# A fused softmax-convolution and cosine FFN on one core: an f32r product moved in every second pair, activation steps of a softmax put in other pairs, and a result tile for each bank at the end

## The chip, the core and the metric

The kernel runs on one core of one Trainium2 chip. The time is device microseconds of one execution, and the median of several runs counts. Engines are named as in the profile: PE (TensorE) with its weight loads PEld, ACT (ScalarE), DVE (VectorE), POOL (GpSimd), SP (the queue that issues DMAs).

## What is computed

For each of 8 sequences of 4,096 tokens with 192 features, a softmax over 7 taps for each of 8 heads weighs the 7 last rows of `x`; the result goes through an FFN with 2,048 hidden features whose activation is `h * cos(h)`. All is f32.

```python
w = exp(weight_gen - max); w = w / (sum(w) + 1e-9)      # softmax over 7 taps, per token and head
x = einsum('bshk,bskhg->bshg', w, windows_of_7_rows(x)) # 32768 x 192
h = x @ w_in                                            # 192 -> 2048
out = (h * cos(h)) @ w_out                              # 2048 -> 192
```

## The kernel before, in words

**Blocks and pairs.** The 32,768 tokens are 64 blocks of 512 (128 partitions times R = 4 rows). The 16 chunks of 128 hidden features make 8 pairs a block, so the main loop (L658) runs over 512 pairs `i`, one in each turn, with `j = i - 8` for the pair whose hidden part is consumed. One turn of the loop is called a period here. What each engine does in a period, and in which order, is the order of the code: the last lines of the kernel chain the instructions of each engine in program order.

**The products on PE.** Each f32 operand is cut in two: an f32r part (`x_hi`, `wa_hi`, `ghi`, `wo`) and a bf16 rest (`x_lo`, `wa_lo`, `glo`), and a product is the sum of the f32r product and of bf16 products of the rests. The contraction over 192 is cut into 128 + 64, and matmuls with 64 rows stand in twos on the two halves of the array. In a period PE does, by function:
- F, `ffn_in_first(i)` (L391): three products of 512 columns into a PSUM tile `h`: `x_lo`, `x_b` (bf16), then `x_hi` (f32r).
- O, `ffn_out(j)` (L468): 16 f32r matmuls `acc<-wo,ghi` of 384 columns, then two transposes (`transpose_row`, L374, `acc<-ident,xa`) of rows of a later block, then 16 bf16 matmuls `acc<-wo_b,glo` of 192 columns.
- the second products, `ffn_in_second(i)` (L406): four bf16 products and two f32r products into `h`.

In even pairs the order is F, O, second. In odd pairs (L682) it is O up to half of its bf16 matmuls (`rest=False`: the `ghi`, the transposes, 8 of the `glo`), then F, then the other 8 `glo` (`rest=True`), then second. `h` has three PSUM buffers, so F of pair `i` needs that `dve_lo(i - 3)` has read the buffer's last content. `acc` has one buffer of two banks; a sum in it takes four periods, k = 0 to 3 with k = i mod 4.

**The other engines.** For each pair ACT makes `turn` from `h` (L427), the cosine (L435) and `ghi` (L445); DVE makes the fraction (L431), the product (L438) and `glo` (L449). `evacuate` (L501) stands behind the products of a period: for k = 1 ACT copies the transposed row out of `acc` (`xrow`, L507) and zeroes its place (L508), for k = 3 it copies the whole `acc` to `part` (L513). The next O that writes `acc` waits for that copy, or for the zeros. In even periods ACT also rounds a row to `x_hi` (L357); POOL makes its `x_b` and `x_lo` (L359, L362).

**The background.** POOL computes the softmax-weighted rows (`attention`, L303), two or three instructions a period. The softmax of 16 rows (4 blocks) is a generator (L231) of which each period takes one step, starting at i mod 32 = 9; its exponential is `powers` (L195): five ACT instructions over 896 columns (L205, L212, L215, L222, L226) with POOL instructions between them, and `wait(n)` counts the periods that are let pass. They come out at i mod 32 = 14, 18, 20, 22 and 26; each stands in ACT's order behind `evacuate` of that period and ahead of `turn` of that pair, which is always an even one.

**The end.** For the last eight values of `j` (L472, `whole`) no F and no second products are left. The last sum, of both banks, lies in one tile (L475); ACT copies 768 columns of it (L513), DVE adds 2 x 192 (L522), and two stores of 96 KB follow (L528).

Of the kernel before, what the change touches and what calls it, by code (L numbers as in the profile page):

```python
# [11 lines left out]
F32 = mybir.dt.float32  # L12
# [4 lines left out]
AF = mybir.ActivationFunctionType  # L17
ALU = mybir.AluOpType
AX = mybir.AxisListType

P = 128
# [24 lines left out]
LN_2 = math.log(2.0)  # L46
ONE_BITS = float(127 * 2 ** 23)
# [3 lines left out]
def tile_softmax_conv_then_cos_ffn(  # L51
# [8 lines left out]
    nc = tc.nc  # L60

    B, S, D = x.shape
# [6 lines left out]
    R = 4  # L69
    NB = RPP // R  # L70
    CT = R * P
# [5 lines left out]
    HALF = NPAIR // 2  # L77
# [9 lines left out]
    work = ctx.enter_context(tc.tile_pool(name="work", bufs=2))  # L87
    ps_h = ctx.enter_context(tc.tile_pool(name="ps_h", bufs=3, space=bass.MemoryType.PSUM))
# [5 lines left out]
    o_v = out.rearrange("(n q r) d -> q n (r d)", n=B, r=RPP)  # L94
# [12 lines left out]
    wa_hi = const.tile([P, F], F32R, name="wa_hi")  # L107
    wa_lo = const.tile([P, F], BF16, name="wa_lo")
    wa_b = tops(wa_hi)
# [4 lines left out]
    wo_b = const.tile([P, NFC, D], BF16, name="wo_b")  # L114
# [80 lines left out]
    def powers(t):  # L195

        (a1, b1), (a2, b2) = EXP_A
        whole_ = work.tile([P, RW * H, K], I32, name="whole", bufs=1)
        side_ = work.tile([P, RW * H, K], F32, name="side", bufs=1)
        whole, side = (v[:, 0:t.shape[1]] for v in (whole_, side_))  # L200

        def wait(n):
            return [None] * n

        nc.scalar.activation(out=whole, in_=t, func=AF.Identity, scale=1.0 / LN_2)  # L205
        yield
        nc.gpsimd.tensor_scalar(
            out=side, in0=whole, scalar1=-LN_2, scalar2=1.0, op0=ALU.mult, op1=ALU.mult)
        nc.gpsimd.tensor_tensor(out=t, in0=side, in1=t, op=ALU.add)
        yield  # L210
        yield from wait(2)
        nc.scalar.activation(out=side, in_=t, func=AF.Square, bias=a1, scale=0.5)  # L212
        yield
        yield from wait(1)
        nc.scalar.activation(out=t, in_=t, func=AF.Square, bias=a2, scale=0.5)  # L215
        yield
        nc.gpsimd.tensor_scalar(
            out=side, in0=side, scalar1=b1, scalar2=1.0, op0=ALU.add, op1=ALU.mult)
        nc.gpsimd.tensor_scalar(
            out=t, in0=t, scalar1=b2, scalar2=1.0, op0=ALU.add, op1=ALU.mult)  # L220
        yield
        nc.scalar.activation(out=whole, in_=whole, func=AF.Relu, bias=ONE_BITS, scale=2.0 ** 23)  # L222
        nc.gpsimd.tensor_tensor(out=t, in0=t, in1=side, op=ALU.mult)
        yield
        yield from wait(3)
        nc.scalar.activation(out=t, in_=t, func=AF.Square)  # L226
        yield
        nc.gpsimd.tensor_tensor(out=t, in0=t, in1=whole.bitcast(F32), op=ALU.mult)
        yield
# [110 lines left out]
    def traded(t):  # L340

        nc.sync.keepalive_nop([nc.sync.lower_ap(t)])  # L342
# [31 lines left out]
    def transpose_row(b, r, acc, s):  # L374

        xa = mixed[b]
        for q in range(2):
            rs = slice(q * D2, (q + 1) * D2)
            nc.tensor.matmul(acc[:, q ^ s, 2 * D + q * D2:2 * D + (q + 1) * D2],  # L379
                             lhsT=xa[rs, r, columns(q ^ s)], rhs=ident[rs, rs], is_transpose=True,  # L380
                             start=False, stop=True, skip_group_check=True)
        if r == R - 1 and s == 1:
            transposed.add(b)
# [4 lines left out]
    def chunk(pair, n):  # L388
        return slice((2 * pair + n) * P, (2 * pair + n + 1) * P)

    def ffn_in_first(i, h=None):  # L391

        b, pair = divmod(i, NPAIR)
        x_hi, x_lo, x_b = xT[b]
        if h is None:
            h = ps_h.tile([P, 2, CT], F32, name="h")
        for m, (w, v) in enumerate(((wa_b, x_lo), (wa_lo, x_b), (wa_hi, x_hi))):
            for q in range(2):
                rs = slice(q * D2, (q + 1) * D2)
                nc.tensor.matmul(  # L400
                    h[:, q, :], lhsT=w[rs, chunk(pair, q)], rhs=v[rs, q, :],
                    start=(m == 0), stop=False, skip_group_check=True)
        hs[i] = h
        traded(h)

# [46 lines left out]
    accs, stores, splits = {}, {}, []  # L452
# [4 lines left out]
    def place(j):  # L457

        b, m = divmod(j, 2 * R)
        tp, k = divmod(m, R)  # L460
        return b, tp, k

    def row_of(j):

        bt, m = divmod(j + LAG - ROWS_AT, 2 * R)
        return (bt + 2, m // 2) if j >= 0 and WHOLE < bt + 2 < NB else None

    def ffn_out(j, rest=None):  # L468

        b, tp, k = place(j)  # L470
        half, s = divmod(k, 2)
        whole = j + LAG >= N  # L472
        if k == 0 and not rest:
            if whole and tp == 1:
                accs[b, tp] = ps_h.tile([P, 2, CT], F32, name="h")  # L475
            else:
                accs[b, tp] = ps_m.tile([P, 2, CT], F32, name="acc")
        acc = accs[b, tp]
        for lo in range(2):
            for c in range(2 * HALF):  # L480
                if rest is not None and rest != (lo == 1 and c >= HALF):
                    continue
                pair, n = divmod(c, 2)
                g = g_parts[b * NPAIR + half * HALF + pair][lo]
                fc = half * 2 * HALF + c
                for q in range(1 if whole else 2):
                    rs = slice(0, P) if whole else slice(q * D2, (q + 1) * D2)
                    bank = q ^ s
                    t = 2 * tp + bank
                    to, w = (acc[:, bank, 0:2 * D], wo) if lo == 0 else (acc[:, bank, 0:D], wo_b)  # L490
                    nc.tensor.matmul(  # L491
                        to, lhsT=g[rs, n, t * P:(t + 1) * P], rhs=w[rs, fc, :],
                        start=(lo == 0 and c == 0 and (k == 0 or whole and k == 1)),
                        stop=(lo == 1 and c == 2 * HALF - 1 and (k == 3 or whole and k == 2)),
                        skip_group_check=True)
            if lo == 0 and not rest and row_of(j):
                transpose_row(*row_of(j), acc, s)
        if k < 3 and not whole and rest is not False:
            traded(acc)

    def evacuate(j):  # L501
        b, tp, k = place(j)
        acc = accs[b, tp]
        row = row_of(j)
        if k == 1 and row:
            t = work.tile([P, 2, P], F32, name="xrow", bufs=1)
            nc.scalar.copy(out=t, in_=acc[:, :, 2 * D:])  # L507
            nc.scalar.copy(out=acc[:, :, 2 * D:], in_=zero.unsqueeze(2).broadcast_to([P, 2, P]))  # L508
        if k == 3:
            accs.pop((b, tp))  # L510
            part = work.tile([P, 2, CT], F32, name="part", bufs=2)
            width = CT if row else 2 * D
            nc.scalar.copy(out=part[:, :, 0:width], in_=acc[:, :, 0:width])  # L513
            t = part[:, :, 2 * D:]
        if k in (1, 3) and row:
            bt, r = row
            splits.append(split(bt, t, slice(r * P, (r + 1) * P), nc.gpsimd))
        if k < 3:
            return
        last = b == NB - 1  # L520
        fin = part[:, :, 0:D]
        (nc.vector if last else nc.gpsimd).tensor_tensor(  # L522
            out=fin, in0=fin, in1=part[:, :, D:2 * D], op=ALU.add)

        def store():
            r0 = b * R + 2 * tp
            for n in range(2):
                nc.sync.dma_start(out=o_v[:, :, (r0 + n) * D:(r0 + n + 1) * D], in_=fin[:, n, :])  # L528

        if last:  # L530
            store()
        else:
            stores[j + LATE] = store
        if tp == 1:
            for pair in range(NPAIR):
                g_parts.pop(b * NPAIR + pair)
# [121 lines left out]
    for i in range(N + LAG + 1):  # L658
# [16 lines left out]
        def products():  # L675
            if b < NB and pair == 0:
                assert b in transposed
            if whole is not None and j >= 0:

                ffn_out(j)  # L680
                ffn_in_first(i, whole)
            elif i < N and j >= 0 and j % 2 != 0:  # L682

                ffn_out(j, rest=False)
                ffn_in_first(i)
                ffn_out(j, rest=True)
            else:
                if i < N:
                    ffn_in_first(i, whole)
                if j >= 0:  # L690
                    ffn_out(j)
            if i < N:
                ffn_in_second(i)
            if j in stores:
                stores.pop(j)()
            if j >= 0:
                evacuate(j)
# [79 lines left out]
```

## Time and profile before

| | |
|---|---|
| median of 3 runs | 2207.42 us (2207.38 to 2207.8) |
| the profiled execution | 2208.1 us, its span 2206.2 us |
| granted TensorE clock | 0.990 over the span |
| busy in the span | PE 2151.6, POOL 2000.7, DVE 1907.6, ACT 1862.9, PEld 1676.4 us |

A row of a timeline tells the start (us from the span's start), the time until the last of the group's instructions ended, engine, line, operation, output and inputs, shapes, and the count; in brackets stands how long the engine was idle before, and what ended that. Consecutive instructions of one kind are one row. The times of matmuls that are in the pipeline together overlap, so what a group costs is read from its start to the start of the next group. A row of a group view tells busy time in us and, behind the comma, the mean ns of one instruction, then the idle time before them.

### The profile page before, as it was taken

What the parts mean: (1) busy time and instruction counts of PE and PEld (TensorE: products, weight loads), DVE (VectorE), ACT (ScalarE), POOL (GpSimd) and SP (SyncE); (2) the same over time, 40 slices, a digit from 0 to 9 for tenths busy, and PEclk for the clock granted to TensorE, in tenths of its full rate; (3) what the DMA queues carried; (4) which work ended last, traced back from release to release, by engine and by line L of the source; (5) the groups of instructions that cost most, each with busy time, mean ns of one, the idle gap of its engine ahead of it and who ended that gap; (6) DMA issues with size and microseconds to landing.
All of it is one profiled execution on the core that took longest, in us unless ns stands there. A gap on an engine that the chain in (4) does not pass through costs nothing.

```text
span 2206.2 us, 62053 instructions
## 1 busy us (share of the span) xinstructions
PE 2151.6 (98%) x26516; PEld 1676.4 (76%) x26516; DVE 1907.6 (86%) x1671; ACT 1862.9 (84%) x2278; POOL 2000.7 (91%) x1687
## 2 busy tenths in 40 slices
PE   4699999999999999999999999999999999999998
PEld 2478777777777777777777777777877777777777
DVE  7888888888888888888888888888888888888886
ACT  4788888888888888888888888888888888888885
POOL 7999999999999999999999999999899999989830
PEclk8799999999999999999999999999999999999999
DMA  7121221221221221221221221211211212211100
GB/s 182 45 48 34 57 48 42 48 48 43 48 57 31 60 48 30 60 48 39 52 48 39 52 56 30 60 46 33 60 41 46 49 41 49 48 40 45 30 16 19
DMA packets 53282, 105.65 MB, mean 48 GB/s; under 512 B 5790, under 2 KB 42134, under 8 KB 53006
## 3 DMA queue, kind: packets, MB, share of 16 engines
q1 hardware_dynamic: 53006, 101.69, 19.3%
q8 instruction: 208, 3.41, 0.7%
q14 instruction: 68, 0.56, 0.1%
HBM read 76.50 MB, written 25.17 MB: 46 GB/s over the span
## 4 chain that ended last, share of the span: by engine, by line
PE 94%; POOL 4%; DVE 1%; issue 1%; DMA 0%; ACT 0%; SPq 0%; POOLq 0%; DVEq 0%; ACTq 0%
PE acc L491 47%; PE h L417 30%; PE h L400 15%; POOL xa L331 1%; PE acc L379 1%; POOL pr L316 1%; PE h L491 0%; POOL wo L154 0%; DMA xt<-in_x_dram 0%; POOL xa L316 0%; POOL wa_lo L154 0%; POOL taps L249 0%; DVE pr L611 0%; POOL taps L281 0%; DVE glo L449 0%
## 5 line engine op out<-in xcount | busy, mean ns | idle before, releaser
L431 DVE TENSOR_TENSOR turn<-h,turn 128x1024 f32<-128x1024 f32 x512 | 627.1, 1225 | 262.8 <-ACT turn L427 258.0
L491 PE MATMUL acc<-wo,ghi 64*128 64x384 f32 x8096 | 808.7, 337 | 0.3 <-ACT ghi L445 0.2
L491 PEld LDWEIGHTS acc<-wo,ghi 64*128 64x128 f32 x8096 | 724.9, 184 | 54.6 <-ACT part L513 16.4
L435 ACT ACTIVATE turn<-turn 128x1024 f32<-128x1024 f32 x512 | 542.4, 1059 | 199.4 <-DVE turn L431 199.3
L331 POOL TENSOR_TENSOR xa<-xa,pr 128x768 f32<-128x768 f32 (+1 forms) x384 | 698.6, 1819 | 0.8
L438 DVE SCALAR_TENSOR_TENSOR h<-h,turn 128x1024 f32<-128x1024 f32 x512 | 631.2, 1233 | 4.6 <-ACT turn L435 4.6
L449 DVE TENSOR_TENSOR glo<-h,ghi 128x1024 bf16<-128x1024 f32 x512 | 622.1, 1215 | 3.8 <-ACT ghi L445 3.8
L427 ACT ACTIVATE turn<-h 128x1024 int32<-128x1024 f32 x512 | 524.6, 1025 | 89.6 <-PE h L417 79.8
L316 POOL TENSOR_TENSOR pr<-xt,taps 128x768 f32<-128x768 f32 (+1 forms) x384 | 589.1, 1534 | 6.3
L445 ACT CAST ghi<-h 128x1024 fp32r<-128x1024 f32 x512 | 516.4, 1009 | 7.5 <-POOL wb_lo L154 5.7
L491 PE MATMUL acc<-wo_b,glo 64*128 64x192 bf16 x8096 | 462.4, 243 | 0.1
L491 PEld LDWEIGHTS <-glo 64*128 64x128 bf16 (+1 forms) x8128 | 317.6, 94 | 85.4 <-issue 67.4
L400 PE MATMUL h<-x_hi,wa_hi 64*128 64x512 f32 x1024 | 300.3, 581 | 0.0
L417 PE MATMUL h<-x_hi,wa_hi 64*128 64x512 f32 x1024 | 300.1, 581 | 0.0
L400 PE MATMUL h<-x_lo,wa_hi 64*128 64x512 bf16 x1024 | 199.2, 384 | 28.6 <-DVE glo L449 20.8
L417 PE MATMUL h<-x_hi,wb_hi 64*128 64x512 f32 x1024 | 204.6, 395 | 0.0
L400 PE MATMUL h<-x_b,wa_lo 64*128 64x512 bf16 x1024 | 196.6, 379 | 2.3 <-POOL wa_lo L154 2.3
L417 PE MATMUL h<-x_lo,wa_hi 64*128 64x512 bf16 x1024 | 195.7, 378 | 2.5 <-SPq L342 1.8
L417 PE MATMUL h<-x_b,wb_lo 64*128 64x512 bf16 x1024 | 195.9, 378 | 0.0
L417 PE MATMUL h<-x_lo,wb_hi 64*128 64x512 bf16 x1024 | 195.9, 378 | 0.0
L417 PE MATMUL h<-x_b,wa_lo 64*128 64x512 bf16 x1024 | 195.9, 378 | 0.0
L359 POOL TENSOR_SCALAR x_b<-x_hi 128x256 bf16<-128x256 f32 (+1 forms) x246 | 102.9, 418 | 93.0 <-ACT x_hi L357 91.7
(90 smaller groups left out, 1973.1 us busy)
## 6 DMA issues: line engine op xcount, KB each, us to landing
xt<-in_x_dram SPq DMA_DIRECT2D x62, 960.0 KB, 7.0
out_dram<-part SPq DMA_DIRECT2D x256, 96.0 KB, 2.2
taps<-in_weight_gen_dram SPq DMA_DIRECT2D x15, 448.0 KB, 4.4
raw<-in_moe_w_out_dram SPq DMA_DIRECT2D x8, 384.0 KB, 9.4
raw<-in_moe_w_in_dram SPq DMA_DIRECT2D x10, 256.0 KB, 11.5
xt<-in_x_dram SPq DMA_DIRECT2D x1, 768.0 KB, 11.5
xt<-in_x_dram SPq DMA_DIRECT2D x1, 540.0 KB, 5.5
raw<-in_moe_w_in_dram SPq DMA_DIRECT2D x4, 128.0 KB, 7.9
```

Source lines behind the costliest of these rows:

```text
L316: eng.tensor_tensor(out=dst.rearrange("p r (h g) -> p r h g", h=H), in0=xt[:, k + ra:k + rb, :].rearrange("p r (h g) -> p r h g", h=H), in ...
L331: eng.tensor_tensor(out=acc if k < K else xa, in0=acc, in1=old[:, ra:rb], op=ALU.add)
L359: nc.gpsimd.tensor_scalar(out=near[:, :, cs], in0=hi[:, :, cs].bitcast(F32), scalar1=1.0, scalar2=1.0, op0=ALU.mult, op1=ALU.mult)
L400: nc.tensor.matmul(h[:, q, :], lhsT=w[rs, chunk(pair, q)], rhs=v[rs, q, :], start=(m == 0), stop=False, skip_group_check=True)
L417: nc.tensor.matmul(h[:, 1 - q, :], lhsT=w[rs, cs], rhs=v[rs, q ^ middle, :], start=False, stop=(m == len(prods) - 1), skip_group_check=True)
L427: nc.scalar.activation(out=t.bitcast(I32), in_=hs[i], func=AF.Identity, bias=0.25, scale=1.0)
L431: nc.vector.tensor_tensor(out=t, in0=hs[i], in1=t.bitcast(I32), op=ALU.subtract)
L435: nc.scalar.activation(out=t, in_=t, func=AF.Sin, bias=SIN_BIAS, scale=SIN_SCALE)
L438: nc.vector.scalar_tensor_tensor(out=hs[i], in0=hs[i], scalar=TWO_PI, in1=turns.pop(i), op0=ALU.mult, op1=ALU.mult)
L445: nc.scalar.copy(out=hi, in_=hs[i])
L449: nc.vector.tensor_tensor(out=lo, in0=hs.pop(i), in1=hi.bitcast(F32), op=ALU.subtract)
L491: nc.tensor.matmul(to, lhsT=g[rs, n, t * P:(t + 1) * P], rhs=w[rs, fc, :], start=(lo == 0 and c == 0 and (k == 0 or whole and k == 1)), st ...
```

## The change

Three parts. In odd pairs, O now stops behind its 16 f32r matmuls; F follows with its f32r product `x_hi` first, then come the transposes, then F's two bf16 products, and then all 16 `glo` matmuls in one piece. In `powers`, the first and the last-but-one kind of ACT step (`whole`, as Identity and as Relu) are cut into two halves of 448 columns, and all steps come out in other periods: halves at i mod 32 = 14, 16, 18 and 22, whole ones at 20, 24 and 28. The POOL instructions that follow them come two to four periods later than before (one of them where it was), the sum and the reciprocal behind them two. At the end the last sum has a tile for each bank, which is copied, added and stored by itself as soon as its bank is done.

The first part moves rows on PE in every odd pair, here in the middle of the program. Before (a MATMUL of f32r loads its weights itself, so only bf16 loads are rows of their own):

```order
L491 MATMUL acc<-wo,ghi 128x384 x16
L379 MATMUL acc<-ident,xa 128x64 x2
L491 LDWEIGHTS glo
L491 MATMUL acc<-wo_b,glo 128x192
...
L400 LDWEIGHTS wa_hi
L400 MATMUL h<-x_lo,wa_hi 128x512
...
L400 MATMUL h<-x_b,wa_lo 128x512
L400 MATMUL h<-x_hi,wa_hi 128x512 x2
L491 LDWEIGHTS glo
L491 MATMUL acc<-wo_b,glo 128x192
```

The same place of the changed kernel, where L413 is F, L513 is O and L389 the transposes:

```order
L513 MATMUL acc<-wo,ghi 128x384 x16
L413 MATMUL h<-x_hi,wa_hi 128x512 x2
L389 MATMUL acc<-ident,xa 128x64 x2
L413 LDWEIGHTS wa_hi
L413 MATMUL h<-x_lo,wa_hi 128x512
...
L413 MATMUL h<-x_b,wa_lo 128x512
L513 LDWEIGHTS glo
L513 MATMUL acc<-wo_b,glo 128x192
```

The `x_hi` product has moved ahead of the transposes, and the two stretches of 8 `glo` matmuls have become one of 16.

The second part moves ACT's steps. Before, at i mod 32 = 14, ACT's order from the rounded row to the next one:

```order
L357 CAST x_hi<-xrow 128x2x128
L205 ACTIVATE whole<-taps 128x896
L427 ACTIVATE turn<-h 128x1024
L445 CAST ghi<-h 128x1024
L435 ACTIVATE turn<-turn 128x1024
L513 COPY part<-acc 128x1024
...
L357 CAST x_hi<-part 128x2x128
L427 ACTIVATE turn<-h 128x1024
```

The same place of the changed kernel (L367 is the rounding, L209 the step, L442, L460 and L450 are `turn`, `ghi` and the cosine, L548 is the copy):

```order
L367 CAST x_hi<-xrow 128x2x128
L209 ACTIVATE whole<-taps 128x448
L442 ACTIVATE turn<-h 128x1024
L460 CAST ghi<-h 128x1024
L450 ACTIVATE turn<-turn 128x1024
L548 COPY part<-acc 128x1024
...
L367 CAST x_hi<-part 128x2x128
L209 ACTIVATE whole<-taps 128x448
L442 ACTIVATE turn<-h 128x1024
```

Only half of the step is left ahead of the copy of `acc`; the other half stands two periods later. A step of full length, at i mod 32 = 20 and likewise at 24 and 28, now stands in a period with k = 0, and what follows it is the copy of a row and the zeros:

```order
L367 CAST x_hi<-part 128x2x128
L223 ACTIVATE side<-taps 128x896
L442 ACTIVATE turn<-h 128x1024
L460 CAST ghi<-h 128x1024
L450 ACTIVATE turn<-turn 128x1024
L533 COPY xrow<-acc 128x256
L534 COPY acc<-zero 128x2x128
```

The diff, cut to what matters:

```diff
+        half = t.shape[1] // 2
+        halves = (slice(0, half), slice(half, 2 * half))
+        for n in range(2):
+            nc.scalar.activation(
+                out=whole[:, halves[n]], in_=t[:, halves[n]], func=AF.Identity, scale=1.0 / LN_2)
+            yield from wait(2 - n)
...
+        def powers_of_2(n):
+            nc.scalar.activation(
+                out=whole[:, halves[n]], in_=whole[:, halves[n]], func=AF.Relu, bias=ONE_BITS, scale=2.0 ** 23)
+        powers_of_2(0)
         yield from wait(2)
         nc.scalar.activation(out=side, in_=t, func=AF.Square, bias=a1, scale=0.5)
         yield
...
+        powers_of_2(1)
+        yield from wait(2)
+        nc.scalar.activation(out=t, in_=t, func=AF.Square, bias=a2, scale=0.5)
...
-    def ffn_in_first(i, h=None):
+    def ffn_in_first(i, h=None, middle=None):
...
+        prods = [(wa_b, x_lo), (wa_lo, x_b), (wa_hi, x_hi)]
+        if middle is not None:
+            prods.insert(0, prods.pop())
...
+            if m == 0 and middle is not None:
+                middle()
...
-                accs[b, tp] = ps_h.tile([P, 2, CT], F32, name="h")
+                accs[b, tp] = [ps_h.tile([P, 2, CT], F32, name="h") for _ in range(2)]
...
-                if rest is not None and rest != (lo == 1 and c >= HALF):
+                if rest is not None and rest != (lo == 1):
...
+        if isinstance(acc, list):
+            if k >= 2:
+                n = k - 2
+                part = work.tile([P, 2, CT], F32, name="part", bufs=2)
+                fin = part[:, 0, 0:D]
+                nc.scalar.copy(out=fin, in_=acc[n][:, 0, D:2 * D])
+                nc.vector.tensor_tensor(out=fin, in0=acc[n][:, 0, 0:D], in1=fin, op=ALU.add)
+                store_rows(b, 2 * tp + n, fin)
+            return
...
                 ffn_out(j, rest=False)
-                ffn_in_first(i)
+                ffn_in_first(i, middle=lambda: rows_of_later(j))
                 ffn_out(j, rest=True)
```

More of the change, by code (lines that the diff above doesn't have):

```diff
@@ L203, in wait @@
             return [None] * n
-        nc.scalar.activation(out=whole, in_=t, func=AF.Identity, scale=1.0 / LN_2)
-        yield
+        half = t.shape[1] // 2
[4 more added lines that the diff above has]
+            yield from wait(2 - n)
         nc.gpsimd.tensor_scalar(
@@ L213, in powers @@
         yield
-        yield from wait(1)
+        nc.gpsimd.tensor_scalar(
+            out=side, in0=side, scalar1=b1, scalar2=1.0, op0=ALU.add, op1=ALU.mult)
+        yield
+        powers_of_2(1)
+        yield from wait(2)
         nc.scalar.activation(out=t, in_=t, func=AF.Square, bias=a2, scale=0.5)
@@ L217, in powers @@
         nc.gpsimd.tensor_scalar(
-            out=side, in0=side, scalar1=b1, scalar2=1.0, op0=ALU.add, op1=ALU.mult)
-        nc.gpsimd.tensor_scalar(
             out=t, in0=t, scalar1=b2, scalar2=1.0, op0=ALU.add, op1=ALU.mult)
-        yield
-        nc.scalar.activation(out=whole, in_=whole, func=AF.Relu, bias=ONE_BITS, scale=2.0 ** 23)
         nc.gpsimd.tensor_tensor(out=t, in0=t, in1=side, op=ALU.mult)
-        yield
         yield from wait(3)
@@ L396, in ffn_in_first @@
             h = ps_h.tile([P, 2, CT], F32, name="h")
-        for m, (w, v) in enumerate(((wa_b, x_lo), (wa_lo, x_b), (wa_hi, x_hi))):
+        prods = [(wa_b, x_lo), (wa_lo, x_b), (wa_hi, x_hi)]
+        if middle is not None:
+            prods.insert(0, prods.pop())
+        for m, (w, v) in enumerate(prods):
             for q in range(2):
@@ L466, in row_of, with rows_of_later @@
         return (bt + 2, m // 2) if j >= 0 and WHOLE < bt + 2 < NB else None
+    def rows_of_later(j):
+        if row_of(j):
+            b, tp, k = place(j)
+            transpose_row(*row_of(j), accs[b, tp], k % 2)
     def ffn_out(j, rest=None):
@@ L478, in ffn_out @@
         acc = accs[b, tp]
+        parted = isinstance(acc, list)
         for lo in range(2):
             for c in range(2 * HALF):
-                if rest is not None and rest != (lo == 1 and c >= HALF):
+                if rest is not None and rest != (lo == 1):
                     continue
@@ L489, in ffn_out @@
                     t = 2 * tp + bank
-                    to, w = (acc[:, bank, 0:2 * D], wo) if lo == 0 else (acc[:, bank, 0:D], wo_b)
+                    to = acc[bank][:, 0] if parted else acc[:, bank]
+                    to, w = (to[:, 0:2 * D], wo) if lo == 0 else (to[:, 0:D], wo_b)
                     nc.tensor.matmul(
@@ L495, in ffn_out, with store_rows @@
                         skip_group_check=True)
-            if lo == 0 and not rest and row_of(j):
-                transpose_row(*row_of(j), acc, s)
+            if lo == 0 and rest is None:
+                rows_of_later(j)
         if k < 3 and not whole and rest is not False:
             traded(acc)
+    def store_rows(b, r, t):
+        r += b * R
+        nc.sync.dma_start(out=o_v[:, :, r * D:(r + 1) * D], in_=t)
     def evacuate(j):
@@ L525, in store @@
         def store():
-            r0 = b * R + 2 * tp
             for n in range(2):
-                nc.sync.dma_start(out=o_v[:, :, (r0 + n) * D:(r0 + n + 1) * D], in_=fin[:, n, :])
+                store_rows(b, 2 * tp + n, fin[:, n, :])
         if last:
```

## The prediction

> **What bounds the kernel now.** I read the page first: busy times, then the chain that ended last.
>
> ```profile
> PE 2151.6 (98%) x26516; PEld 1676.4 (76%) x26516; DVE 1907.6 (86%) x1671; ACT 1862.9 (84%) x2278; POOL 2000.7 (91%) x1687
> PE 94%; POOL 4%; DVE 1%; issue 1%; DMA 0%; ACT 0%; SPq 0%; POOLq 0%; DVEq 0%; ACTq 0%
> ```
>
> PE is busy nearly always and carries the chain. So only two things can shorten the time: fewer us of PE work, or fewer moments in which PE waits. The chain in order of time tells how regular these are. Its rows (start, duration) recur.
>
> ```profile
> 1087.54 1.60 PE acc L491 x12
> 1220.61 1.61 PE acc L491 x10
> ...
> 2021.94 1.42 PE acc L491 x16
> ...
> 2096.34 1.42 PE acc L491 x16
> ```
>
> The first two are the same place in two successive groups of 32 periods (one softmax each): 133.07 us. The last two lie where no softmax is left: 74.40 us, which is 18 periods of 4.133 us, so 32 quiet periods would take 132.27 us. A group with a softmax loses 0.80 us. The view of waits names the loss:
>
> ```profile
> PEld acc L491 <- ACT part L513: 16.4, 57, 0.6
> PEld acc L491 <- ACT acc L508: 2.9, 14, 0.2
> ```
>
> 57 is four in each of 14 groups and one more, 14 is one in each: five waits a group, as many as there are ACT steps in `powers`. (The idle time of weight loads is more than what is lost, since a load may come early.) 14 x 0.80 = 11.2 us are lost this way; all else in the middle is PE's own work.
>
> **PE's work in an odd pair.** The timeline of PE over one quiet odd pair and the end of the next even one, and the weight loads that go with it:
>
> ```profile
> 1165.32 0.40 PE L417 MATMUL h<-x_hi,wb_hi 64*128 64x512 f32 x2
> 1165.55 1.58 PE L491 MATMUL acc<-wo,ghi 64*128 64x384 f32 x16
> 1166.97 0.22 PE L379 MATMUL acc<-ident,xa 64*128 64x64 f32 x2
> 1167.02 0.49 PE L491 MATMUL acc<-wo_b,glo 64*128 64x192 bf16 x8
> 1167.35 0.38 PE L400 MATMUL h<-x_lo,wa_hi 64*128 64x512 bf16 x2
> 1167.57 0.38 PE L400 MATMUL h<-x_b,wa_lo 64*128 64x512 bf16 x2
> 1168.02 0.50 PE L491 MATMUL acc<-wo_b,glo 64*128 64x192 bf16 x8
> 1168.36 0.38 PE L417 MATMUL h<-x_lo,wa_hi 64*128 64x512 bf16 x2
> ...
> 1169.69 0.39 PE L400 MATMUL h<-x_lo,wa_hi 64*128 64x512 bf16 x2
> ...
> 1171.83 0.82 PE L491 MATMUL acc<-wo_b,glo 64*128 64x192 bf16 x16
> 1172.49 0.38 PE L417 MATMUL h<-x_lo,wa_hi 64*128 64x512 bf16 x2
> ```
>
> ```profile
> 1165.32 1.48 PEld L491 LDWEIGHTS acc<-wo,ghi 64*128 64x128 f32 x16
> ...
> 1168.01 0.28 PEld L491 LDWEIGHTS <-glo 64*128 64x128 bf16 x8 [0.25 <-issue]
> ```
>
> From start to start: 0.22 us for a bf16 product of 512 columns (1167.35 to 1167.57), 0.23 for an f32r one with f32r behind it (1165.32 to 1165.55), 0.45 for `x_b` and `x_hi` together (1167.57 to 1168.02), which is 0.22 + 0.23: the f32r load costs nothing behind bf16. Eight `glo` take 0.33 behind the transposes (1167.02 to 1167.35) but 0.34 behind `x_hi` (1168.02 to 1168.36); there the bf16 loads stood still for 0.25 us until the f32r stream had ended. Sixteen in one piece take 0.66 (1171.83 to 1172.49).
>
> Before, from the transposes to the second products: 0.05 + 0.33 + 0.22 + 0.45 + 0.34 = 1.39 us. After: `x_hi` 0.23, transposes 0.05, `x_lo` 0.22, `x_b` 0.22, `glo` 0.66: 1.38 us. The switch from f32r to bf16 behind `x_hi` goes away, since the transposes stand there now. That is 0.01 us a pair; the pairs are i = 9 to 511, odd, without 13 (there F uses another tile): 251 of them, so **2.5 us** less. Bounds: nothing at the least, and twice the rounding of the rows, 0.025 us, at the most: 0 to 6.3 us. A loss is a rival below.
>
> The Trainium skill bears on this, in "TensorE: Matmul & The Clock Gate", Part 3, "The mechanism": the PE pulls a weight load ahead of matmuls in flight whenever it goes to other rows of the array or to the background buffer. By that rule the order of types would cost nothing, and this term would be 0 instead of 2.5. The trace disagrees at one place, the 0.25 us above; so I go by the row.
>
> What hides the move: F starts 0.38 us earlier in odd pairs. It needs a buffer of `h` that DVE's `glo` has read:
>
> ```profile
> 1167.96 1.22 DVE L449 TENSOR_TENSOR glo<-h,ghi 128x1024 bf16<-128x1024 f32 x1
> ```
>
> It ends at 1169.18, and the even pair's F starts at 1169.69: 0.51 us of slack. A period (4.13) earlier it ended at 1165.05, and the odd pair's F started at 1167.35: 2.3 us, of which 1.9 is left. The queues that the product is moved past have none of its data; SP only gets its notice of F earlier relative to the second products (0.66 us ahead instead of 0.34).
>
> **ACT's steps.** ACT's timeline, with PE's starts of the second products as marks:
>
> ```profile
> 1169.04 0.99 ACT L513 COPY part<-acc 128x1024 f32<-128x1024 f32 x1
> ...
> 1173.23 0.39 ACT L357 CAST x_hi<-part 128x256 fp32r<-128x256 f32 x1
> 1174.03 1.03 ACT L427 ACTIVATE turn<-h 128x1024 int32<-128x1024 f32 x1 [0.41 <-PE h L417]
> ...
> 1177.70 0.38 ACT L508 COPY acc<-zero 128x256 f32<-128x256 f32 x1
> ...
> 1181.45 0.39 ACT L357 CAST x_hi<-xrow 128x256 fp32r<-128x256 f32 x1
> 1181.74 0.95 ACT L205 ACTIVATE whole<-taps 128x896 int32<-128x896 f32 x1
> 1182.60 1.00 ACT L427 ACTIVATE turn<-h 128x1024 int32<-128x1024 f32 x1
> ...
> 1185.86 0.99 ACT L513 COPY part<-acc 128x1024 f32<-128x1024 f32 x1
> ```
>
> ```profile
> 1176.62 0.38 PE L417 MATMUL h<-x_lo,wa_hi 64*128 64x512 bf16 x2
> ...
> 1184.89 0.38 PE L417 MATMUL h<-x_lo,wa_hi 64*128 64x512 bf16 x2
> ...
> 1189.14 0.38 PE L417 MATMUL h<-x_lo,wa_hi 64*128 64x512 bf16 x2
> ```
>
> I count from the mark ahead. In a quiet period with k = 3 the copy runs from +0.68 to +1.67, and the next mark comes after 4.13 us. After the step it runs from +0.97 to +1.96, and the next mark comes after 4.25: PE lost 0.12, so it waits when the copy (or the zeros) ends later than about +1.84. The zeros of a quiet k = 1 period end at +1.46. Slack: 0.17 for k = 3, 0.38 for k = 1.
>
> A whole step takes 0.86 us to the next start (1181.74 to 1182.60). A half costs more than half; the same activation at 448 columns stands in the groups of ACT kept apart by shape:
>
> ```profile
> L253 ACT ACTIVATE taps<-taps 128x448 f32<-128x448 f32 x1 | 0.6, 578 | 1.1 <-POOL taps L249 1.1
> ```
>
> That is 0.58, or 0.49 to the next start by the same overlap of 0.09. A half: for k = 0, `x_hi` starts at +0.74, takes 0.29 to the next start, the half ends at +1.52; `turn` would wait for PE until +1.54 (1174.03). So halves delay nothing, at k = 2 neither, where all starts 0.04 earlier. A whole step at k = 0: 0.74 + 0.29 + 0.86 = +1.89, so `turn` is 0.35 late. What is late next? The zeros of the next period, at most at 1.46 + 0.35 = +1.81, under 1.84; DVE's `glo`, 0.35 of 0.51; then ACT catches up, since the period of k = 2 leaves 0.4 idle and carries no step or half of one. So all five waits go and none comes: **11.2 us** less, with 0.03 us of margin at three places a group. Bounds: if each whole step still costs the 0.12 of now, 3 x 14 x 0.12 = 5.0 come back, so 6.2 to 11.2.
>
> POOL's turn: the first half of the Relu step now overwrites `whole` a period after POOL's read is issued (17, 18).
>
> ```profile
> 1188.03 0.94 POOL L207 TENSOR_SCALAR side<-whole 128x896 f32<-128x896 int32 x1
> ...
> 1191.13 1.54 POOL L316 TENSOR_TENSOR pr<-xt,taps 128x768 f32<-128x768 f32 x1
> ...
> 1197.12 1.83 POOL L331 TENSOR_TENSOR xa<-xa,pr 128x768 f32<-128x768 f32 x1
> ```
>
> That read now stands behind six more POOL rows, from the one at 1191.13 to the one at 1197.12, which take 7.8 us; so it starts near 1195.8 and ends near 1196.8. The half would start near the mark of period 18 plus 1.0, that is 1189.14 + 2 x 4.13 + 1.0 = 1198.4. Margin 1.6 us; cost nothing.
>
> **The end.** The last copy and sum of two banks:
>
> ```profile
> 2200.79 0.80 ACT L513 COPY part<-h 128x768 f32<-128x768 f32 x1 [7.64 <-PE h L491]
> 2201.62 0.56 DVE L522 TENSOR_TENSOR part<-part 128x384 f32<-128x384 f32 x1 [7.88 <-ACT part L513]
> ```
>
> ```profile
> L528 SPq DMA_DIRECT2D out_dram<-part x256: 537/591/1212, 116.3 to 2202.8; - x128
> ```
>
> One bank is left at the end: the copy shrinks from 768 columns (0.80) to 192, which by the slope between 0.39 for 256 and 0.80 for 768 is 0.34; the sum from 384 to 192 columns, between half of 0.56 and all of it, I take 0.35; and one store follows instead of two, so that a second issue (median 0.59) is gone. 0.46 + 0.21 + 0.59 = **1.3 us** less; bounds 0.6 (the store's issue alone) to 1.8.
>
> **The sum.** 2.5 + 11.2 + 1.3 = 15.0 us off the profiled execution's 2208.1 gives 2193.1. The median of the runs is 0.7 under that execution, so 2192.4 us is the forecast. By the bounds it lies between 2207.4 - 19.3 = 2188.1 and 2207.4 - 6.8 = 2200.6. A measurement of this kernel can tell about 0.2% (4.4 us) from no change.
>
> **The rivals.**
>
> *ACT's whole steps still hold PE up.* For it: the margin is 0.03 us. Against: 0.35 is the lateness at its first place, and some of it is lost on the way (`turn` at +1.85 made the copy 0.29 late, not 0.31). With 5.0 us back: 2197.4 us.
>
> *The order of types on PE is free*, so that 2.5 is 0: 2194.9 us. For it: 0.01 us is the rounding of the rows. Against: the loads that stood still for 0.25. It is what the Trainium skill's rule above would give.
>
> *The f32r loads come into the open: slower.* In odd pairs `x_hi` waits for DVE and stands behind f32r matmuls; the only loads that waited in such a place are the bf16 ones above, which weren't pulled ahead. An f32r load takes 0.19 us at most (16 in 1.48, two at a time). If it isn't hidden under the last `ghi` matmul, 251 x 0.19 = 47.7 us come on top: 2240.1 us. It decides from 15.0 / 251 = 0.06 us a pair. Against: the f32r load of the first `ghi` started with the last f32r product (both at 1165.32) and was hidden.
>
> *The change does not do what it says*, since ACT's first Relu half waits for POOL: every us by which POOL is later than my 1.6 us of margin is lost by ACT in each of 14 groups. At 1 us of loss of PE a group the 11.2 would be made up: about 2206 us. Against: POOL's instructions are as many as before, in almost the same order.
>
> **How the numbers follow.** The forecast with all three terms 0.74; ACT's rest 0.11; types free 0.08; slower 0.04; POOL 0.03. The likeliest time is 2192.4. For 8 in 10 I take 2189 to 2199: the forecast with most of its bounds and the first two rivals, 0.93 together, less what lies in the outer bounds. Faster by over 0.2% (under 2203.0) are the first three, less a little: 0.92; POOL's case is within 0.2%, with that little: 0.04; slower 0.04.
>
> **What would show it right or wrong.** Odd pairs: from the last `ghi` to the second products 1.38 us behind one `x_hi` of 0.23, all 16 `glo` in 0.66, and no idle load ahead of `glo`. ACT: no wait of PE's loads for the copy (57 now) or the zeros (14); a group of 32 periods in 132.3 - 16 x 0.01 = 132.1 us in the chain, not 133.1. POOL: no wait of ACT for it at the Relu half. The end: one store behind the last sum, 1.3 us less from PE's end to the end of the span. A copy or zeros that still release PE would show the first rival, an idle f32r load in odd pairs the third; then I am wrong in that term.

## The result, and the profile after

The changed kernel takes 2192.8 us (median of 5 runs, 2192.63 to 2193.29), the kernel before 2207.42 beside it (5 runs, 2207.24 to 2207.8): a ratio of 0.9934 (95% interval 0.9923 to 0.9945), or 14.6 us less. The profiled execution took 2193.29 us, its span 2191.4, at a granted clock of 0.989. The forecast was 2192.4; as will be seen, two of its terms were off in opposite directions.

The page, in the two lines that were shown of before:

```profile
PE 2138.7 (98%) x26516; PEld 1691.5 (77%) x26516; DVE 1906.2 (87%) x1672; ACT 1863.0 (85%) x2309; POOL 2001.1 (91%) x1687
PE 93%; POOL 4%; DVE 1%; issue 1%; DMA 0%; ACT 0%; SPq 0%; POOLq 0%; DVEq 0%; ACTq 0%
```

PE is busy for 12.9 us less with as many instructions, and still bounds the kernel. ACT has 31 instructions more (two halves for one step, twice in 15 softmaxes, and one more copy at the end) and is busy as long as before, 0.1 us apart. The chain in order of time (start, duration):

```profile
1072.81 1.41 PE acc L513 x16
...
1204.86 1.42 PE acc L513 x16
...
1934.53 1.41 PE acc L513 x16
...
1984.01 1.41 PE acc L513 x16
```

The first two are one group apart: 132.05 us, where it was 133.07. The last two lie where no softmax is left: 49.48 us for 12 periods, 4.123 each, so 32 quiet periods take 131.95 (132.27 before). So a group gained 1.02 us, 0.32 of it PE's own work in 16 odd pairs (0.020 each) and 0.70 the waits for ACT. Averaged over the groups behind the first, from the starts of the second products, a softmax now costs 0.086 us where it cost 0.79. The waits:

```profile
PEld acc L513 <- ACT acc L534: 2.7, 15, 0.2
PEld L513 <- issue: 2.5, 15, 0.3
...
PEld acc L513 <- ACT part L548: 1.4, 3, 0.6
...
ACT whole L218 <- POOL side L212: 0.8, 1, 0.8
```

57 waits for the copy became 3: two in the first group, at its pairs 16 and 20, and one at i = 512, where no F is left. The zeros still release PE's loads: once in each of 14 groups, always behind the whole step at i mod 32 = 24, and once more in the first group, behind the one at 20. And ACT waits once for POOL at the Relu half, which the forecast held not to happen.

**PE in an odd pair.** The timeline of PE, to be held against the odd pair of before:

```profile
1001.87 1.57 PE L513 MATMUL acc<-wo,ghi 64*128 64x384 f32 x16
1003.28 0.39 PE L413 MATMUL h<-x_hi,wa_hi 64*128 64x512 f32 x2
1003.51 0.22 PE L389 MATMUL acc<-ident,xa 64*128 64x64 f32 x2
1003.57 0.38 PE L413 MATMUL h<-x_lo,wa_hi 64*128 64x512 bf16 x2
1003.78 0.38 PE L413 MATMUL h<-x_b,wa_lo 64*128 64x512 bf16 x2
1004.00 0.82 PE L513 MATMUL acc<-wo_b,glo 64*128 64x192 bf16 x16
1004.66 0.38 PE L432 MATMUL h<-x_lo,wa_hi 64*128 64x512 bf16 x2
```

And the weight loads of that pair:

```profile
1003.11 0.19 PEld L413 LDWEIGHTS h<-x_hi,wa_hi 64*128 64x128 f32 x2
...
1003.52 0.10 PEld L413 LDWEIGHTS <-wa_hi 64*128 64x128 bf16 x2
```

From `x_hi` to the second products it is 1003.28 to 1004.66, the forecast 1.38. The `ghi` stretch ahead of it takes 1.41 (1001.87 to 1003.28) where it took 1.42 with the transposes behind it. In ns, as means over the quiet odd pairs of the two traces, the first stretch went from 1389 to 1378 and the `ghi` from 1417 to 1409: together 0.019, with the rest of the pair 0.020 us. The load of `x_hi` (1003.11 to 1003.30) runs under the last `ghi` matmuls, and ends 0.02 us behind the start of `x_hi`. In the middle of the program no load ahead of `glo` stands still any more; the 15 that are left lie in the first 111 us and behind 2130 us.

**ACT around whole steps and a half.** The timeline of ACT from the whole step at 20 to the zeros behind the one at 24, and PE's starts of the second products as marks:

```profile
1199.61 0.95 ACT L223 ACTIVATE side<-taps 128x896 f32<-128x896 f32 x1
...
1204.12 0.38 ACT L534 COPY acc<-zero 128x256 f32<-128x256 f32 x1
...
1207.99 0.57 ACT L218 ACTIVATE whole<-whole 128x448 int32<-128x448 int32 x1
...
1211.74 1.00 ACT L548 COPY part<-acc 128x1024 f32<-128x1024 f32 x1
...
1216.21 0.95 ACT L230 ACTIVATE taps<-taps 128x896 f32<-128x896 f32 x1
...
1220.71 0.38 ACT L534 COPY acc<-zero 128x256 f32<-128x256 f32 x1
```

```profile
1202.69 0.38 PE L432 MATMUL h<-x_lo,wa_hi 64*128 64x512 bf16 x2
...
1210.95 0.38 PE L432 MATMUL h<-x_lo,wa_hi 64*128 64x512 bf16 x2
...
1219.21 0.38 PE L432 MATMUL h<-x_lo,wa_hi 64*128 64x512 bf16 x2
```

Behind the whole step at 20 the zeros end at 1204.50, +1.81 from their mark, as was worked out; behind the half at 22 (0.57) the copy starts at +0.79 and ends at +1.79. Behind the whole step at 24 the zeros end at 1221.09, +1.88, and PE's load waits for them:

```profile
1221.14 1.36 PEld L513 LDWEIGHTS acc<-wo,ghi 64*128 64x128 f32 x16 [0.17 <-ACT acc L534]
```

That is the wait that is left in each group. Behind the halves at 14 and 18, with no whole step two periods ahead of them, the copy ends at +1.70 (median of the groups) as in a quiet period. So ACT is late behind 24 because it had not yet made up the steps at 20 and 22; the runs on POOL's wait below bear this out.

**The first group.** ACT's timeline there:

```profile
135.06 0.58 ACT L218 ACTIVATE whole<-whole 128x448 int32<-128x448 int32 x1 [0.82 <-POOL side L212]
...
138.81 0.99 ACT L548 COPY part<-acc 128x1024 f32<-128x1024 f32 x1
```

and POOL's read of `whole`, here and in a later group, each with the row that differs most ahead of it:

```profile
118.38 2.02 POOL L369 TENSOR_SCALAR x_b<-x_hi 128x1024 bf16<-128x1024 f32 x1
...
134.09 0.94 POOL L212 TENSOR_SCALAR side<-whole 128x896 f32<-128x896 int32 x1
...
1174.99 0.41 POOL L369 TENSOR_SCALAR x_b<-x_hi 128x256 bf16<-128x256 f32 x1 [2.10 <-ACT x_hi L367]
...
1188.52 0.95 POOL L212 TENSOR_SCALAR side<-whole 128x896 f32<-128x896 int32 x1
```

In the later group the read ends at 1189.47, and the half that overwrites `whole` starts at 1191.30: 1.8 us of margin. In the first group POOL is that much later and 0.8 more. The copy of `acc` then ends at 139.80, +2.51 from its mark (137.29), and PE's period there takes 4.805 us, in the trace of before 4.25. POOL's rows show a part of the reason: in the first group it makes the `x_b` of a whole block (2.02 us where the later group has 0.41), and no idle time of it is shown from 108 us to this read, while in the later group it still waited 2.10 us for ACT. That this is all of it was not tried.

**The end**, as the timeline of all engines shows it:

```profile
2187.23 0.32 ACT L540 COPY part<-h 128x192 f32<-128x192 f32 x1 [1.75 <-PE h L513]
2187.59 0.36 DVE L541 TENSOR_TENSOR part<-h,part 128x192 f32<-128x192 f32 x1 [1.71 <-ACT part L540]
```

0.32 for the copy (forecast 0.34), 0.36 for the sum (0.35), and one store behind it. From the last start of second products to the end of the span it is 23.73 us, 25.03 before: 1.30 less.

**The balance.** 251 x 0.020 = 5.0 from PE's order, 14 x 0.70 = 9.8 from the waits, 1.3 at the end; against it 0.7 where POOL is late and 0.5 by which the first second products start later (27.00 us, 26.54 before; this start lies between 25.6 and 27.5 in the profiles of all kernels here, so it isn't the change's). That makes 14.9 of the 14.8 us between the spans (2206.2 and 2191.4).

### The profile page after: what moved, and what is told of

Read it like the earlier page. It is cut to its first block, busy times and chain, and to the rows that moved or that the text cites. A ratio compares the mean times of both kernels' runs of the same rounds, so it can differ in the third digit from the quotient of the medians.

```text
span 2191.4 us, 62216 instructions
## 1 busy us (share of the span) xinstructions
PE 2138.7 (98%) x26516; PEld 1691.5 (77%) x26516; DVE 1906.2 (87%) x1672; ACT 1863.0 (85%) x2309; POOL 2001.1 (91%) x1687
## 4 chain that ended last, share of the span: by engine, by line
PE 93%; POOL 4%; DVE 1%; issue 1%; DMA 0%; ACT 0%; SPq 0%; POOLq 0%; DVEq 0%; ACTq 0%
PE acc L513 47%; PE h L432 30%; PE h L413 15%; POOL xa L341 2%; POOL pr L326 1%; PE acc L389 1%; PE h L513 0%; POOL wo L154 0%; DMA xt<-in_x_dram 0%; POOL xa L326 0%; POOL wa_lo L154 0%; POOL taps L259 0%; DVE glo L464 0%; DVE pr L645 0%; POOL taps L291 0%
## 5 line engine op out<-in xcount | busy, mean ns | idle before, releaser
L513 PE MATMUL acc<-wo,ghi 64*128 64x384 f32 x8096 | 800.8, 335 | 0.3 <-ACT ghi L460 0.2
L513 PEld LDWEIGHTS acc<-wo,ghi 64*128 64x128 f32 x8096 | 727.4, 184 | 45.0 <-ACT acc L534 2.7
L450 ACT ACTIVATE turn<-turn 128x1024 f32<-128x1024 f32 x512 | 541.5, 1058 | 198.9 <-DVE turn L446 198.7
L442 ACT ACTIVATE turn<-h 128x1024 int32<-128x1024 f32 x512 | 524.7, 1025 | 75.4 <-PE h L432 69.5
L460 ACT CAST ghi<-h 128x1024 fp32r<-128x1024 f32 x512 | 516.9, 1010 | 7.3 <-POOL wb_lo L154 5.6
L513 PE MATMUL acc<-wo_b,glo 64*128 64x192 bf16 x8096 | 419.0, 243 | 0.1
L513 PEld LDWEIGHTS <-glo 64*128 64x128 bf16 (+1 forms) x8128 | 341.5, 94 | 71.4 <-issue 2.5
L432 PE MATMUL h<-x_hi,wa_hi 64*128 64x512 f32 x1024 | 299.6, 581 | 0.0
L413 PE MATMUL h<-x_hi,wa_hi 64*128 64x512 f32 x1024 | 253.2, 491 | 0.0
L413 PE MATMUL h<-x_lo,wa_hi 64*128 64x512 bf16 x1024 | 198.2, 383 | 29.2 <-DVE glo L464 21.4
L413 PE MATMUL h<-x_b,wa_lo 64*128 64x512 bf16 x1024 | 195.5, 378 | 1.9 <-POOL wa_lo L154 1.9
L557 POOL TENSOR_TENSOR part<-part 128x384 f32<-128x384 f32 x126 | 128.6, 1021 | 54.3 <-ACT part L548 46.8
```

Of the source, the lines that this page charges most:

```text
L413: nc.tensor.matmul(h[:, q, :], lhsT=w[rs, chunk(pair, q)], rhs=v[rs, q, :], start=(m == 0), stop=False, skip_group_check=True)
L432: nc.tensor.matmul(h[:, 1 - q, :], lhsT=w[rs, cs], rhs=v[rs, q ^ middle, :], start=False, stop=(m == len(prods) - 1), skip_group_check=True)
L442: nc.scalar.activation(out=t.bitcast(I32), in_=hs[i], func=AF.Identity, bias=0.25, scale=1.0)
L450: nc.scalar.activation(out=t, in_=t, func=AF.Sin, bias=SIN_BIAS, scale=SIN_SCALE)
L460: nc.scalar.copy(out=hi, in_=hs[i])
L513: nc.tensor.matmul(to, lhsT=g[rs, n, t * P:(t + 1) * P], rhs=w[rs, fc, :], start=(lo == 0 and c == 0 and (k == 0 or whole and k == 1)), st ...
```

## The experiments

Theory: three gains that hardly touch each other: the order of types on PE, ACT's late steps, the end. Rivals: the types are free and only the waits went; the move works by where `x_hi`'s load lies, not by the types; cutting the steps matters or only their place. Each run stands beside the kernel before on the same chip: 2207.45 us (27 runs) for the first four, 2207.68 (9) for the next four, 2207.99 (9) for the last two.

**The three parts, each alone** on the kernel before. The order of PE:

```diff
-                if rest is not None and rest != (lo == 1 and c >= HALF):
+                if rest is not None and rest != (lo == 1):
...
                 ffn_out(j, rest=False)
-                ffn_in_first(i)
+                ffn_in_first(i, middle=lambda: rows_of_later(j))
                 ffn_out(j, rest=True)
```

> The order on PE alone; exponential steps and end as before. Theory: what an odd pair gains does not depend on the other parts. The changed kernel's trace has odd periods shorter by 0.020 us (0.011 behind the last ghi product of O, 0.008 between the ghi products and what follows them), so 251 x 0.020 = 5.0 us less than before: about 2202.4 us, with the five waits a group for ACT still there (57 and 14). As the prediction had it, 0.010 a pair: 2204.9 us. Rival, the order of types is free on PE: no difference, 2207.4 us.

Measured: 2204.36 us (2203.89 to 2204.85), 0.9986 (0.9977 to 0.9995): 3.1 less. The waits:

```profile
PEld acc L503 <- ACT part L525: 16.9, 57, 0.6
...
PEld L503 <- issue: 2.8, 17, 0.3
PEld acc L503 <- ACT acc L520: 2.8, 14, 0.2
```

In the kernel before, the row of the idle loads was

```profile
PEld L491 <- issue: 67.4, 275, 0.3
```

The idle loads ahead of `glo` went from 275 to 17, and the quiet odd pairs are as short as in the changed kernel (4.118 us), which is worth 5.0. But the waits for ACT are all there, and longer: a softmax now costs 0.89 us instead of 0.79. Such a wait ends when ACT ends, so what PE saves ahead of it is waited away: 14 x 0.10 = 1.4 us. The types are not free; the result lies between the two numbers for that reason.

The exponential's steps, with the new `powers` of the change and nothing else:

> The exponential steps alone; PE's order and the end as before. Theory: the waits for the copy of acc and for the zeros go by themselves, 14 groups x 0.70 us, less 0.7 us that ACT loses once, in the first group, waiting for POOL: 9.1 us less, about 2198.3 us, odd periods unchanged. Rival, that the waits went because PE's order gave the copy more room: no more than a third of it, 2204 us or more.

Measured: 2198.17 us (2198.03 to 2198.31), 0.9958 (0.9945 to 0.997): 9.3 less, as expected. The waits:

```profile
PEld L501 <- issue: 67.5, 273, 0.3
...
PEld acc L501 <- ACT part L523: 1.4, 3, 0.5
...
ACT whole L218 <- POOL side L212: 0.8, 1, 0.8
...
PEld acc L501 <- ACT acc L518: 0.4, 2, 0.2
```

PE's idle loads are untouched; the waits for ACT are gone but for those of the first group and the last pair, for the zeros too (2, not 15). With the longer odd pairs of before, the zeros end earlier behind their marks (medians: +1.76 behind 20 and 28, +1.81 behind 24; in the change +1.80 and +1.88), and +1.81 is still in time. A softmax costs 0.028 us here. The wait for POOL comes with this part.

The tile for each bank, with `evacuate` of the change for the last sum:

> The end alone: a tile for each bank of the last sum. Theory: copy 0.80 to 0.32, sum 0.56 to 0.36, one store's issue of 0.6 gone: 1.3 us less, about 2206.1 us, all of it behind PE's last matmul. Rival, that only the second store's issue counts: 0.6 us less, 2206.8 us.

Measured: 2206.16 us (2205.89 to 2206.66), 0.9994 (0.9985 to 1.0003): 1.3 less, as expected, though that interval holds no change; the tail of its own trace, 23.72 us against 25.03, says more. The parts make 3.1 + 9.3 + 1.3 = 13.7, the change 14.6. The difference fits what the order's gain loses when ACT's waits stay (1.4) less what the steps lose when the odd pairs get shorter (14 x 0.058 = 0.8), but at 0.9 us it is within the intervals of these ratios.

**Which rows of the order matter.** In the changed kernel the transposes put back straight behind `ghi`, `x_hi` behind them and still first of F:

```diff
-                ffn_in_first(i, middle=lambda: rows_of_later(j))
+                rows_of_later(j)
+                ffn_in_first(i, middle=lambda: None)
```

> The changed kernel with the two transposes put back straight behind the ghi products in odd pairs: ghi, transposes, x_hi, x_lo, x_b, glo in one piece. Theory: the transposes between x_hi and x_lo are what hides the switch from f32r to bf16; without them the bf16 load waits again until the f32r stream has ended (about 0.012 us) and the step from the ghi products to the transposes costs 0.008 more than to x_hi: odd periods as long as before the change, 251 x 0.020 = 5.0 us more than the changed kernel, about 2197.8 us. If only the switch counts: 2195.8 us. Rival, that the gain came from glo in one piece or that types are free: 2192.8 us as the changed kernel.

Measured: 2212.41 us (2212.08 to 2212.67), 1.0022 (1.0013 to 1.0031): slower than before, and all three expectations missed. PE's timeline and its loads:

```profile
1169.75 0.22 PE L389 MATMUL acc<-ident,xa 64*128 64x64 f32 x2
1169.77 0.48 PE L413 MATMUL h<-x_hi,wa_hi 64*128 64x512 f32 x2
1170.10 0.39 PE L413 MATMUL h<-x_lo,wa_hi 64*128 64x512 bf16 x2
```

```profile
1169.75 0.19 PEld L413 LDWEIGHTS h<-x_hi,wa_hi 64*128 64x128 f32 x2
1170.09 0.10 PEld L413 LDWEIGHTS <-wa_hi 64*128 64x128 bf16 x2 [0.16 <-issue]
```

The load of `x_hi`, 0.19 us, now starts with the transposes, which in the change take only 0.06 us from their start to the next (1003.51 to 1003.57), too short to cover it. From the transposes to `x_lo` it takes 0.35 (1169.75 to 1170.10); in the changed kernel the same two products take 0.29 (1003.28 to 1003.57). That is 0.060 of the 0.081 us by which the odd pair is longer (4.199); 0.012 more are the switch to bf16 behind `x_hi` (the loads idle 0.16), 0.008 the `ghi` stretch. 251 x 0.081 = 20.3 us, measured 19.6. So this is the prediction's rival of f32r loads in the open, at 0.06 instead of 0.19 us a pair. The change escapes it because `x_hi` stands ahead of the transposes, behind the `ghi` matmuls, under which its load is hidden. The order of types has its part as well: of the change's 0.020 us a pair, 0.012 is the switch to bf16 that the transposes hide, and 0.008 the shorter `ghi` stretch.

F in its old order behind the transposes, and only `glo` in one piece:

```diff
-                ffn_in_first(i, middle=lambda: rows_of_later(j))
+                rows_of_later(j)
+                ffn_in_first(i)
```

> The changed kernel with F of odd pairs in its old order behind the transposes: ghi, transposes, x_lo, x_b, x_hi, glo in one piece. The trace of the run before this one showed that x_hi straight behind the transposes pays 0.060 us a pair for its weight load, which the short transposes don't cover. Here x_b covers it. Theory: what is left against the changed kernel is the switch behind x_hi (0.012) and the step from the ghi products to the transposes (0.008): odd periods as long as before the change, 251 x 0.020 = 5.0 us more than the changed kernel, about 2197.8 us. Rival, that the gain is in glo in one piece: 2192.8 us.

Measured: 2198.2 us (2198.18 to 2199.12), 0.9957 (0.9944 to 0.9971): `glo` in one piece alone brings nothing. The waits row of the loads is that of before:

```profile
PEld L513 <- issue: 67.5, 266, 0.3
```

Odd pairs take 4.143 us; against the change that is 0.025, with the same matmuls in another order. By the rule of the Trainium skill in "TensorE: Matmul & The Clock Gate", Part 3, "The mechanism" (a load for other rows or the background buffer is pulled ahead), the loads of `glo` would cost nothing behind `x_hi` either. The trace disagrees at the 266 loads that stood still: the 16 `glo` behind them take 0.671 us where they take 0.660 in the change (means over the quiet odd pairs).

**The new order in even pairs as well:**

```diff
-            elif i < N and j >= 0 and j % 2 != 0:
+            elif i < N and j >= 0:
```

> The changed kernel with the odd pairs' order in even pairs too, from pair 8 on. Theory: in even pairs F ahead of O is the time in which ACT copies acc (k = 0) or zeroes its row (k = 2). Without it the ghi products would start at +1.33 us behind the second products' start, and the copy ends at +1.67, the zeros at +1.46: waits of about 0.4 and 0.2 us in every four periods, 128 x 0.6 = 77 us more: 2260 to 2290 us. Rival, that the switch of types is what counts in even pairs too: about 250 x 0.02 = 5 us less than the changed kernel, 2188 us.

Measured: 2288.86 us (2 runs, 2288.26 and 2289.45), 1.0368 (1.0349 to 1.0387). The waits:

```profile
PEld acc L513 <- ACT part L548: 86.4, 126, 0.8
PEld acc L513 <- ACT acc L534: 55.5, 122, 0.5
```

Even pairs that wait for the copy take 0.51 us more, those that wait for the zeros 0.28. In even pairs F, 0.68 us long, stands between the second products and O, and it is the cover of ACT's copies: without it O would write `acc` from +1.16 on by the limit of the prediction (1.84 less 0.68), and the copy ends at +1.67, the zeros at +1.46: 0.51 and 0.30. 126 pairs of each make 102 us, less 252 x 0.02 = 5 from the order: 97; measured 96 more than the change. The expected 77 us were too little, since they counted to the start of `ghi` (+1.33) and not to that limit.

**Cut or only moved.** The Identity and the Relu as whole steps at 14 and 22:

```diff
-        for n in range(2):
-            nc.scalar.activation(
-                out=whole[:, halves[n]], in_=t[:, halves[n]], func=AF.Identity, scale=1.0 / LN_2)
-            yield from wait(2 - n)
+        nc.scalar.activation(out=whole, in_=t, func=AF.Identity, scale=1.0 / LN_2)
+        yield from wait(3)
```

> The changed kernel with the two steps on whole not cut: Identity whole at i mod 32 = 14, Relu whole at 22, the other three as changed. Theory: a whole step ahead of the copy of acc (k = 2) makes the copy end 0.29 late, 0.12 past what PE allows; the one at 22 comes behind a late period too and costs 0.2 to 0.3. 14 x 0.35 = 4.9 us more, less the 0.7 of the first group's wait for POOL, which has no cause here: about 2197.0 us. Rival, that only the three steps' new place matters, and cutting is for nothing: 2192.8 us or, without the halves' own cost, 2192.0.

Measured: 2199.1 us (2198.77 to 2199.75), 0.9962 (0.9949 to 0.9974). The waits:

```profile
PEld acc L509 <- ACT part L544: 9.4, 29, 0.6
...
PEld acc L509 <- ACT acc L530: 2.9, 14, 0.2
```

The two uncut steps bring two waits a group back, and a softmax costs 0.62 us instead of 0.086. So the cut is worth 6.3 us of the 9.8. (The wait of ACT for POOL is gone here too, so that the waits for ACT alone cost some 7.) The expected 4.2 was too small: the whole step at 22 costs 0.31 us at its copy, and the zeros behind the one at 24 another 0.11.

**The wait for POOL.** The Relu halves at 22 and 26 instead of 18 and 22:

```diff
-        powers_of_2(0)
         yield from wait(2)
...
-        powers_of_2(1)
+        powers_of_2(0)
...
-        yield from wait(3)
+        yield
+        powers_of_2(1)
+        yield from wait(2)
```

> The changed kernel with the two Relu halves at i mod 32 = 22 and 26 instead of 18 and 22. Theory: the wait of ACT for POOL's read of whole, at pair 18 of the first group alone, goes, and with it 0.7 us of PE; the half at 26 stands behind the whole step at 24 and makes the copy end at about +1.85, 0 to 0.03 us past the limit a group: 2192.1 to 2192.6 us. Rival, that the first group is late for another reason (the ramp's POOL work): 2192.8 us, with the same period 19 to 20.

Measured: 2193.16 us (2192.84 to 2193.29), 0.9934 (0.9922 to 0.9947): no gain. ACT no longer waits for POOL; but the waits have

```profile
PEld acc L514 <- ACT acc L535: 5.3, 28, 0.2
```

28 where the change has 15: the whole step at 28, two periods behind the half at 26, is now late at its zeros in each group (0.08 us). ACT has not made up the half's time by then: the zeros behind 28 end at +1.93 (median of the groups), in the change, where nothing stands at 26, at +1.80. Behind 24 it is the same: +1.88 where a half stands at 22, and +1.95 in the run before this one, with the whole step there. A softmax costs 0.168 us. With the second half at 30, behind the last Square (`yield from wait(2)`, `powers_of_2(1)`, `yield`), and the changed kernel again beside it:

> The changed kernel with the two Relu halves at i mod 32 = 22 and 30 instead of 18 and 22: none behind POOL's read of whole, none between the whole steps at 24 and 28. Theory: the first group's 0.7 us goes as in the run before this one, and the 0.08 us a group that the half at 26 cost there (it made the whole step at 28 late) does not come: 2192.1 us, and no wait of PE after pair 30 of a group. Rival, that a half behind a whole step costs wherever it stands: 2193.2 us as the run before.

> The changed kernel once more, beside the run above on the same chip: 2192.8 us; the wait of ACT for POOL in the first group is there again (0.8 us), since it follows from the order. If it is not, it was chance.

Measured: 2192.46 us (2191.7 to 2192.61), 0.9929 (0.9916 to 0.9941), and for the changed kernel 2192.99 (2192.88 to 2193.33), 0.9932 (0.9919 to 0.9946). The waits of the first:

```profile
PEld acc L514 <- ACT acc L535: 2.1, 12, 0.2
```

and of the changed kernel again:

```profile
ACT whole L218 <- POOL side L212: 0.8, 1, 0.8
```

The wait for POOL comes again with the order and goes with it; a softmax costs 0.077 us, and the 12 waits for the zeros that are left all stand behind the step at 24. The five runs of each don't overlap, and lie 0.5 us apart, near the 0.7 that the wait costs in the trace. It is the best version here; against the change it is below what this measurement can tell by ratio.

## Why the prediction was right, step by step

- **PE's order: right in its cause, half of it in size.** 2.5 us were forecast, 5.0 came. The stretch behind `ghi` was right (0.011 for 0.01 a pair); the step that failed is that the `ghi` stretch ahead of it was taken as unchanged. It ends at another neighbour, `x_hi` instead of the transposes, and is 0.008 shorter. Both lie inside the bounds of 0 to 6.3, which rows of two decimals forced.
- **ACT's five waits: 9.8 for 11.2; the limit was right, the catching up was not.** The waits for the copy went, but for two in the first group and one at the end. The limit of +1.84 held: in these traces the end of a late copy or of late zeros, less what PE lost there, is +1.84 or +1.85 (medians: +1.96 and 0.115 for a copy before, +1.88 and 0.03 for the zeros now). The step that failed is "then ACT catches up, since the period of k = 2 leaves 0.4 idle and carries no step or half of one": 22 is such a period, and the change puts a half there. So only two of the "three places a group" have the zeros of +1.81; behind 24 they end at +1.88, and there stand 14 of the 15 waits. The shorter odd pairs took margin too: with the old order of PE (the steps alone) the same zeros end at +1.81 and cost no wait. Most of the rest of the 0.086 lies at pairs 22, 24 and 30 of a group, about 0.01 at each, where no load is shown to wait for ACT. The trace of before had the sign of it: of its 0.79 us a softmax, 0.35 lie at the copy behind the step at 22, two periods behind the step at 20, and only 0.12 or less at each of the other four. The rival that charged 0.12 at each of three places a group is out: it would be 0.36 a group, and 0.086 is left.
- **POOL's read "cost nothing": wrong once.** The margin of 1.6 us is right where it was read (1.8), and wrong in the first group, where POOL is later: 0.7 us. The rival named the place and the mechanism; it held in one group of 14.
- **The end: 1.30 for 1.3.**
- **Types free: out**, by the order alone and by `glo` in one piece. **f32r loads in the open:** not in the change (no idle ahead of its load), but the run with the transposes back shows the mechanism at 0.060 us a pair, just at the 0.06 from which it would have decided.
- **The sum:** 15.0 forecast, 14.6 measured between the medians. That it came so close is luck, since errors of both signs met: 2.5 too little for PE's order, against 1.4 too much for ACT's waits, 0.7 for POOL and 0.5 for the scatter of the start.

What stays open: whether POOL's larger `x_b` explains all of its lateness in the first group, the scatter of the start, and the 0.01 us at each of three pairs weren't tried. The exact limit of the copy and the zeros was read from waits, not measured by itself.

## What to carry to other kernels

Price a moved matmul by both its neighbours and by its weight load: a load wants a stream in front of it that lasts about as long (here 0.19 us was hidden behind `ghi` matmuls that come every 0.18 us in twos, and not behind transposes of 0.06), and a row that is harmless in one place (a short transpose) uncovers it in another. Where PE waits for an engine at a fixed time, a saving on PE is waited away, so the late engine's step goes first, or both together (the order alone lost some 1.4 of its 5.0 us that way). A margin is to be checked for each step with the steps just ahead of it, with the periods as short as the change makes them, and in the first group as well as in a steady one.

## What was not expected of the hardware

- An f32r load of 128 columns takes 0.19 us, a bf16 one 0.10. Behind a 384-column f32r matmul the f32r load costs nothing; with only two 64-column transposes to cover it, 0.060 us a pair came into the open.
- Bf16 loads behind an f32r product stand still for 0.16 to 0.25 us, but cost only about 0.012 us each time; with fp32 transposes between, neither is seen.
- The same work needs 0.008 us less in a stretch of 16 f32r matmuls when an f32r product and not a transpose follows.
